# Attended blocks turned on VectorE instead of passing through DRAM, in a sliding-window transformer block

## The chip, the cores and the metric

The kernel runs on one core of a Trainium2 chip. A core has TensorE for matrix products (PE in the profile, PEld for its weight loads), VectorE (DVE), ScalarE (ACT), GpSimd (POOL) and SyncE (SP), which issues most transfers. Sixteen DMA engines move the data. The engines run their own instruction streams in order and wait for each other through semaphores. The metric is the device time of one execution in microseconds; three runs of the kernel before gave 324.6, 325.6 and 327.06 us, a median of 325.6.

## The reference

One block of a transformer with 2048 tokens of 640 features, everything in bf16. A small condition vector `c` gives six vectors of shift, scale and gate:

```python
mod = (_silu(c) @ w_mod).reshape(c.shape[0], 6, 1, -1)
sa, ca, ga, sb, cb, gb = (mod[:, i] for i in range(6))
h = _layernorm(x, axis=-1) * (1 + ca) + sa
x = x + ga * _A_ref(h, A_wqkv, A_wo)
h = _layernorm(x, axis=-1) * (1 + cb) + sb
x = x + gb * _B_ref(h, B_w_gate, B_w_up, B_w_down)
```

`_A_ref` is attention with 32 heads of 20 features. A query sees itself and the 255 keys before it:

```python
qkv = (x @ wqkv).reshape(B, S, 3, H, Dh).transpose(2, 0, 3, 1, 4)
scores = jnp.einsum('bhqd,bhkd->bhqk', q, k) * Dh ** (-0.5)
mask = (idx[:, None] - idx[None, :] >= 0) & (idx[:, None] - idx[None, :] < 256)
p = softmax(where(mask, scores, -1e9))
o = jnp.einsum('bhqk,bhkd->bhqd', p, v)
return o.transpose(0, 2, 1, 3).reshape(B, S, D) @ wo
```

`_B_ref` is a gated MLP with 1536 hidden features: `(sigmoid(x @ w_gate) * (x @ w_up)) @ w_down`.

## The kernel before

The tokens are worked on in 8 chunks of 256, each of two blocks of 128 rows. A chunk `a` goes through these steps:

- `ln1` norms its rows and brings them into `hT`, features on partitions. For chunks 0 and 1 the turn is made on TensorE (line 686, operand `ident`), from chunk 2 on by a DMA that transposes (line 810). The modulation by `ca` and `sa` follows on ScalarE, VectorE or GpSimd (lines 819 to 828).
- `qkv` multiplies `hT` by wq, wk and wv (line 686). Copies out of PSUM (`evac`, lines 902 and 903) put queries and keys into `stg` with each head of 20 padded to 32 columns, and values into `V` with a stride of 22, the last two columns being ones. `stg` is turned into `QT` and `KT`, on TensorE for chunks 0 and 1, else by DMA.
- `attention` runs over two halves `q` of 16 heads. A set of scores (line 687, `S<-QT,KT`) fills four PSUM banks, ScalarE takes the exponential (`L1054`, `L1028`), GpSimd clears what lies outside the window (`L1032`, `L1059`, `L1063`). A PV product (`burst`, line 687, `M<-E,V`) gives two PSUM banks with 16 heads of 20 features and the sum of weights as row 20, heads on partitions in groups of 32. It is issued ahead of a later set of scores, with one half's delay (`pend`).
- `close` ends a half. `norm` (line 1146) turns both banks into `T1` in 32 x 32 blocks on VectorE (L1150), takes reciprocals (L1155), divides into `Tn` (L1157), and turns `Tn` back into `On` (L1159), heads on partitions. Heads of 20 rows in groups of 32 are not the dense 128 rows that the output product needs. So four DMAs write `On` to a DRAM tensor `doc` and one DMA reads `doc` back into `oT`, tiles 0 and 1 after the first half, 2 to 4 after the second.
- `outproj` multiplies `oT` by `wo` (line 686, `M<-wo,oT`), adds the residual (L1240), norms, turns by DMA into `h2T` and modulates. `wo` had been multiplied by the gate `ga` beforehand (L1331), `wd` by `gb` (L1268).
- `mlp` is gate and up products (`M<-h2T,wg` and `M<-h2T,wu`), tanh on ScalarE (L1285), the product on VectorE (L1287), and the down product (`M<-wd,hh`), residual (L1306) and store.

The order of the work is fixed beforehand. Every operation is recorded by `A(...)` with its engines, a cost and the tiles that it reads and writes. `PLAN` is a list of numbers: a number divided by 5 is the operation's place in the recording, the remainder its engine (PE, ACT, DVE, POOL, SP). `schedule` walks the list once, checks that what an operation needs has come before, gives tiles their buffers and keeps each engine's order as listed. `emit` writes the five streams with their semaphores. The costs in microseconds in the calls decide only which buffer a tile takes; a search that is not part of the kernel made the list. All transfers but a few that are listed for ScalarE's queue are issued by SP in its listed order, so one that waits holds those behind it.

Buffers matter to the change: `Tn`, `On`, `T1`, `Dr` and `oT` have one buffer each, and PSUM tiles `M` have four banks. Tn's padding is cleared once on GpSimd (L599).

Of the kernel before, what the change touches and what calls it, by code (L numbers as in the profile page):

```python
# [348 lines left out]
def c_pe(n):  # L349
# [118 lines left out]
]  # L468
TR1 = 2
NPH = 2  # L470
NPQ = 2
PQ = ()
# [913 lines left out]
```

## Time and profile before

| | |
|---|---|
| runs of the kernel before | 324.6, 325.6, 327.06 us |
| the profiled execution | 326.74 us |
| its span, first to last instruction | 324.8 us |
| granted TensorE clock | 1.0 |
| TensorE busy | 316.1 us (97%) |
| ScalarE, VectorE, GpSimd busy | 213.0, 205.6, 188.0 us |
| DMA traffic | 38.20 MB, of that HBM read 21.30 and written 5.25 |

A line of a group reads: line of the kernel, engine, operation, tile written <- tiles read, shapes, count, then busy microseconds and the mean nanoseconds of one, then the engine's idle time before these instructions and what ended it. A wait reads: who waited, for whom, microseconds in total, times, the longest. A stretch reads: from, to, length, then for each engine its busy time and its number of instructions. A row of the timeline or of the chain begins with its start and its length. SPq and ACTq are issues of transfers on a queue.

### The profile page before, as it was taken

The page shows a single profiled execution, that of the slowest core. Times are in us where ns is not written, and L with a number is a line of the kernel's source. Part 1 is how long each engine was busy: PE and PEld are TensorE (multiplying, and loading weights), DVE is VectorE, ACT ScalarE, POOL GpSimd, SP SyncE. Part 2 cuts the span into 40 slices and gives each one's busy share as a digit, 9 for nine tenths or more (in the row PEclk, how much of TensorE's full clock was granted, in tenths as well). Part 3 has the DMA queues.
Part 4 walks back from the last instruction along what each step waited for, and adds up shares of the span by engine and source line. Part 5 has one row for each costly group of instructions (what it writes and reads, how often), then busy time and mean ns, then how long its engine had stood idle before and what let it go on. Part 6 is the DMA issues. An engine that isn't in the chain of part 4 may idle for free.

```text
span 324.8 us, 11997 instructions
## 1 busy us (share of the span) xinstructions
PE 316.1 (97%) x5044; PEld 236.8 (73%) x5045; DVE 205.6 (63%) x426; ACT 213.0 (66%) x228; POOL 188.0 (58%) x349
## 2 busy tenths in 40 slices
PE   6999999989999999999999999999999999999996
PEld 2666767667776777776787777777888777887885
DVE  4699987768686865674755647464845376645423
ACT  2699984788678877988685857676886756320220
POOL 5337858855868677948774846676583958001000
PEclk9999999999999999999999999999999999999999
DMA  7999989998648464726551303465121206112201
GB/s 238 370 315 245 281 161 189 207 192 281 186 91 140 64 139 75 109 60 130 118 71 26 83 2 73 126 65 120 39 47 28 77 22 83 38 46 41 83 0 42
DMA packets 73023, 38.20 MB, mean 118 GB/s; under 512 B 46602, under 2 KB 71690, under 8 KB 72970
## 3 DMA queue, kind: packets, MB, share of 16 engines
q1 hardware_dynamic: 71808, 36.13, 50.6%
q10 hardware_dynamic: 1162, 1.31, 1.5%
q8 instruction: 40, 0.66, 0.9%
q14 instruction: 13, 0.11, 0.1%
HBM read 21.30 MB, written 5.25 MB: 82 GB/s over the span
## 4 chain that ended last, share of the span: by engine, by line
PE 76%; DVE 0%; issue 0%
PE M L686 64%; PE S L687 6%; PE M L687 5%; DVE x L1306 0%
## 5 line engine op out<-in xcount | busy, mean ns | idle before, releaser
L1054 ACT ACTIVATE E<-S 128x2048 bf16<-128x2048 f32 x56 | 105.0, 1876 | 45.7 <-PE S L687 45.4
L1063 POOL TENSOR_SCALAR_AFFINE_SELECT E<-E 128x512 bf16<-128x512 bf16 x112 | 69.6, 635 | 8.4 <-DVE Tn L1157 2.1
L1059 POOL TENSOR_SCALAR_AFFINE_SELECT E<-E 128x256 bf16<-128x256 bf16 x112 | 45.4, 415 | 48.3 <-PE M L686 14.8
L686 PE MATMUL M<-h2T,wu 128*128 128x256 bf16 x480 | 68.0, 273 | 0.5 <-DVE h2T L828 0.5
L686 PE MATMUL M<-h2T,wg 128*128 128x256 bf16 x480 | 67.0, 273 | 0.0
L686 PE MATMUL M<-wd,hh 128*128 128x320 bf16 (+2 forms) x396 | 57.3, 296 | 0.0
L1287 DVE SCALAR_TENSOR_TENSOR hh<-sig,M 128x512 bf16<-128x512 f32 x48 | 32.2, 680 | 34.9 <-ACT sig L1285 24.1
L686 PEld LDWEIGHTS M<-h2T,wu 128*128 128x128 bf16 x480 | 45.3, 98 | 8.4 <-issue 0.7
L686 PEld LDWEIGHTS M<-h2T,wg 128*128 128x128 bf16 x480 | 45.5, 98 | 6.9 <-DVE T L1150 0.2
L686 PEld LDWEIGHTS M<-wd,hh 128*128 128x128 bf16 x396 | 37.0, 98 | 14.0 <-DVE hh L1287 0.2
L1285 ACT ACTIVATE sig<-M 128x512 f32<-128x512 f32 x48 | 28.2, 596 | 27.7 <-PE M L686 27.1
L1032 POOL TENSOR_SCALAR_AFFINE_SELECT E<-E 128x1024 bf16<-128x1024 bf16 x28 | 31.9, 1144 | 6.8 <-DVE st L781 2.5
L1306 DVE TENSOR_TENSOR x<-M,x 128x320 bf16<-128x320 f32 (+2 forms) x33 | 15.7, 479 | 29.4 <-PE M L686 28.9
L687 PE MATMUL S<-QT,KT 20*64 20x256 bf16 (+5 forms) x1856 | 32.3, 228 | 1.3 <-issue 0.7
L687 PEld LDWEIGHTS S<-QT,KT 20*64 20x64 bf16 (+1 forms) x1856 | 20.0, 100 | 18.4 <-issue 8.8
L781 DVE BATCH_NORM_STATS2 st<-x 128x6 f32<-128x320 bf16 x64 | 28.9, 477 | 1.3 <-DMA x<-in_A_x_dram 1.0
L1150 DVE STREAM_TRANSPOSE T<-M 128x512 f32<-128x512 f32 x32 | 21.4, 698 | 13.1 <-PE S L687 10.5
L1028 ACT ACTIVATE E<-S 128x2048 bf16<-128x2048 f32 x14 | 26.3, 1876 | 5.1 <-PE S L687 5.0
L686 PE MATMUL M<-wq,hT 128*128 128x320 bf16 x160 | 25.9, 300 | 1.5 <-ACT hT L827 0.9
L686 PE MATMUL M<-wv,hT 128*128 128x320 bf16 x160 | 26.8, 300 | 0.0
L686 PE MATMUL M<-wk,hT 128*128 128x320 bf16 x160 | 26.2, 300 | 0.0
L686 PE MATMUL M<-wo,oT 128*128 128x320 bf16 x160 | 24.8, 300 | 0.0
(86 smaller groups left out, 362.7 us busy)
## 6 DMA issues: line engine op xcount, KB each, us to landing
x<-in_A_x_dram SPq DMA_DIRECT2D x19, 160.0 KB, 8.4
doc<-On SPq DMA_DIRECT2D x64, 40.0 KB
out_dram<-x SPq DMA_DIRECT2D x14, 160.0 KB, 1.8
wd<-in_w_mod_dram SPq DMA_DIRECT2D x6, 320.0 KB
wd<-in_B_w_down_dram SPq DMA_DIRECT2D x4, 480.0 KB
wu<-in_w_mod_dram SPq DMA_DIRECT2D x5, 320.0 KB
oT<-doc SPq DMA_DIRECT2D x8, 192.0 KB
wg<-in_B_w_gate_dram SPq DMA_DIRECT2D x2, 576.0 KB
```

Source lines behind the costliest of these rows:

```text
L686: return e.matmul(o, l, r, start=st, stop=sp, skip_group_check=True)
L687: return e.matmul(o, l, r, start=st, stop=sp, tile_position=tp, skip_group_check=True)
L781: A("dve", lambda e, g, bi=bi, j=j: e.bn_stats(v(bi * 12 + j * 6, 6), src[bi].ap[:, j * 320:(j + 1) * 320]), 0.48, reads=[src[bi].r()], wr ...
L1028: A("act", lambda e, eng: e.activation(cell().rearrange("p m (x c) -> p m x c", c=64)[:, :, 0:4:3, :], Sp.ap[:].rearrange("p j (k x c) -> ...
L1032: A("pool", lambda e, eng, c0=c0, pat=pat, base=base, cm=cm: e.affine_select(cell()[:, :, c0:c0 + 64], cell()[:, :, c0:c0 + 64], pattern=p ...
L1054: A("act", lambda e, eng: e.activation(part(0, 512), Sp.ap[:], ACT.Exp, scale=SM_SCALE), 1.876, reads=[Sp.r()], writes=[E.r("C"), E.r("B") ...
L1059: A("pool", lambda e, eng, hc=hc, src=src, far_h=far_h: e.affine_select(side(hc), part(src, 64), pattern=[[0, 4], [-1 if far_h else 1, 64] ...
L1063: A("pool", lambda e, eng, c0=c0, near=near: e.affine_select(part(c0, 128), part(c0, 128), pattern=[[0, 4], [1 if near else -1, 128]], com ...
L1150: A("dve", lambda e, g, h=h: e.transpose(T1.ap[:, 512 * h:512 * h + 512], X[h].ap), 0.694, reads=[X[h].r()], writes=[T1.r(h)], prio=3.5, t ...
L1285: A("act", lambda e, g, pg=pg, sg=sg: e.activation(sg.ap[:], pg.ap[:], ACT.Tanh, scale=0.5), c_act(512), reads=[pg.r()], writes=[sg.r()], ...
L1287: A("dve", lambda e, g, pu=pu, sg=sg, f0=f0: e.scalar_tensor_tensor(out=hh.ap[:, f0:f0 + 2, :], in0=sg.ap[:].rearrange("p (a b) -> p a b", ...
L1306: A("dve", lambda e, g, ps=ps, bi=bi, c0=c0, n=n: e.tensor_tensor(x1[bi].ap[:, c0:c0 + n], ps.ap[:, 0:n], x1[bi].ap[:, c0:c0 + n], op=ALU. ...
```

## The change

`On`, `doc`, the four writes and the read of each half go. A half now only turns, takes reciprocals and divides; the divide writes into one `Tn` of 1280 columns for the whole chunk, ordered by block of 32 queries, then head, then feature, without padding. After the second half two turns on VectorE, one for each block of 128 rows, write straight into `oT`. For this the heads are dealt differently: head `16q + 4j + k` lies in partition group `j`, so that the 160 features of a group are five dense tiles of 32 rows. The copies of queries and keys into `stg` write the heads in this order, and `wo` is loaded with its rows permuted alike, by eight DMAs in place of one. The output product waits for `oT` by block of rows and for `wo` by tile. The clearing of `Tn` goes. The costs of `ends` and `score` change, and `PLAN` is a new list that differs from about the tenth microsecond on: 2089 operations instead of 2163.

```diff
 PLAN = [
...
-TR1 = 2
...
-    p_Tn = sbpool("Tn", 1, [128, 1024])
-    p_On = sbpool("On", 1, [128, 1024])
+    p_Tn = sbpool("Tn", 1, [128, 1280])
...
-    for i in range(len(p_Tn.aps)):
-        p_Tn.init[i].append(A("pool", lambda e, g, i=i: e.memset(p_Tn.aps[i][:], 0.0), 1.0, writes=[R("ti")], prio=3))
...
-    dma(lambda: wo[:], lambda: A_wo.rearrange("(t p) f -> p t f", p=128), 2.15, writes=[R_wo], prio=0.5, tag="wo")
+    for t in range(NDT):
+        if t == 2:
+            for j in range(4):
+                dma(lambda j=j: wo[32 * j:32 * j + 32, 2, :],
+                    lambda j=j: A_wo.rearrange("(u e) f -> u e f", e=16)[5 * j + 4:5 * j + 21:16], 0.11, writes=[R_wo[2][j]], prio=0.5,
+                    tag="wo")
+        else:
+            dma(lambda t=t: wo[:, t, :],
+                lambda t=t: A_wo.rearrange("(q j e) f -> q j e f", q=2, j=4)[t // 3][:, (32 * t) % 80:(32 * t) % 80 + 32, :], 0.43,
+                writes=R_wo[t], prio=0.5, tag="wo")
...
-                        evac(lambda s=s, half=half: heads(s.ap[:, half * 512:half * 512 + 512], 32)[:, :, 0:DH],
-                             lambda ps=ps: heads(ps.ap[:, 0:320], DH), 320, [ps.r()], [s.r(half)], 6, f"evqk{a}")
+                        evac(lambda s=s, half=half: s.ap[:, half * 512:half * 512 + 512].rearrange(
+                            "p (k j x) -> p j k x", k=4, x=32)[:, :, :, 0:DH],
+                             lambda ps=ps: ps.ap[:, 0:320].rearrange("p (j k d) -> p j k d", j=4, d=DH), 320, [ps.r()], [s.r(half)], 6, f"evqk{a}")
...
-        last["s"] = [with_pv(f"ends{a}", sc, 0.29, set_reads(a, q), [G, Sp], before, 1)]
+        last["s"] = [with_pv(f"ends{a}", sc, 0.25, set_reads(a, q), [G, Sp], before, 1)]
...
-        last["s"] = [with_pv(f"score{a}", sc, 0.25, set_reads(a, q), [E, Sp], before, 3)]
+        last["s"] = [with_pv(f"score{a}", sc, 0.262, set_reads(a, q), [E, Sp], before, 3)]
...
-                        h = 4 * (4 * q + k) + j
+                        h = 16 * q + 4 * j + k
...
-    def norm(X, On, a):
-        T1, Tn, Dr = Tile(p_T1, "T1"), Tile(p_Tn, "Tn"), Tile(p_Dr, "Dr")
+    def norm(X, Tn, q, a):
+        T1, Dr = Tile(p_T1, "T1"), Tile(p_Dr, "Dr")
...
-        A("dve", lambda e, g: e.tensor_tensor(blk(Tn), blk(T1), Dr.ap[:].unsqueeze(2).to_broadcast([128, 32, DH]), op=ALU.mult),
-          0.82, port=True, reads=[T1.r(0), T1.r(1), Dr.r()], writes=[Tn.r()], prio=4, tag=f"divide_{a}")
-        A("dve", lambda e, g: e.transpose(On.ap[:], Tn.ap[:]), 1.22, reads=[Tn.r()], writes=[On.r()], prio=4, tag=f"tr2_{a}")
+        A("dve", lambda e, g: e.tensor_tensor(
+            Tn.ap[:].rearrange("p (b k d) -> p k b d", k=8, d=DH)[:, 4 * q:4 * q + 4],
+            T1.ap[:].rearrange("p (k b r) -> p k b r", k=4, r=32)[:, :, :, 0:DH],
+            Dr.ap[:].rearrange("p (k b) -> p k b", k=4).unsqueeze(3).to_broadcast([128, 4, 8, DH]), op=ALU.mult),
+          0.82, port=True, reads=[T1.r(0), T1.r(1), Dr.r()], writes=[Tn.r(q)], prio=4, tag=f"divide_{a}")
...
-            On = Tile(p_On, f"On{a}_{q}")
-            norm(X, On, a)
-            for j in range(4):
-                Rj = R(f"doc{a}_{q}_{j}")
-                dma(lambda j=j, q=q: rdoc[j * DH:(j + 1) * DH, 4 * q:4 * q + 4, :],
-                    lambda j=j, On=On: On.ap[32 * j:32 * j + DH, :].rearrange("p (g c) -> p g c", g=4), 0.22,
-                    reads=[On.r()], writes=[Rj], prio=1, tag=f"n_ow_{a}", dur=0.42)
-                R_doc[q].append(Rj)
-            t0, t1 = ((0, 2), (2, 5))[q]
-            dma(lambda t0=t0, t1=t1: oT.ap[:, t0:t1, :], lambda t0=t0, t1=t1: doc.rearrange("(t p) c -> p t c", p=128)[:, t0:t1, :],
-                0.41, reads=R_doc[0] + (R_doc[1] if q else []), writes=[oT.r(q)], prio=1.5, tag=f"oT_{a}", dur=0.5, dlat=2.88)
+            norm(X, Tn, q, a)
             if q == 1:
+                for bi in range(2):
+                    A("dve", lambda e, g, bi=bi: e.transpose(
+                        oT.ap[:, :, bi * 128:bi * 128 + 128].rearrange("p t (b c) -> p b t c", c=32), Tn.ap[:, 640 * bi:640 * bi + 640]),
+                      0.83, reads=[Tn.r(0), Tn.r(1)], writes=[oT.r(bi)], prio=4, tag=f"tr2_{a}")
...
-                pe_chain(ps, 320, pairs, [[oT.r(0 if t < 2 else 1), R_wo] for t in range(NDT)], 15, f"wo{a}",
+                pe_chain(ps, 320, pairs, [[oT.r(bi)] + R_wo[t] for t in range(NDT)], 15, f"wo{a}",
...
-          reads=[R_wo, R_gbc], writes=[R_wo], prio=20, tag="wos")
+          reads=R_wo[t] + [R_gbc], writes=R_wo[t], prio=20, tag="wos")
```

More of the change, by code (lines that the diff above doesn't have):

```diff
@@ L562, in build @@
     R_w3 = {k: [R(k + "0"), R(k + "1")] for k in ("wq", "wk", "wv")}
-    R_crow, R_ident, R_ccol, R_cth, R_siluc, R_silubc, R_wo = (R(n) for n in ("crow", "ident", "ccol", "cth", "siluc", "silubc", "wo"))
+    R_crow, R_ident, R_ccol, R_cth, R_siluc, R_silubc = (R(n) for n in ("crow", "ident", "ccol", "cth", "siluc", "silubc"))
+    R_wo = [[R(f"wo{t}{i}") for i in range(4 if t == 2 else 1)] for t in range(NDT)]
     R_wg = [[R(f"wg{t}_{h}") for t in range(NDT)] for h in range(2)]
@@ L1130, in pv @@
                     for j in range(4):
-                        h = 4 * (4 * q + k) + j
+                        h = 16 * q + 4 * j + k
                         ins = mm(e, X[bank].ap[32 * j:32 * j + 32, oc:oc + n * 128], V[2 * a + kb].ap[:, h * VW:h * VW + 32],
@@ L1144, in burst @@
         return a, pv, (6 if a else 3) * 512 / 2400.0 * 1.04 + 0.02, rd, X
-    def norm(X, On, a):
-        T1, Tn, Dr = Tile(p_T1, "T1"), Tile(p_Tn, "Tn"), Tile(p_Dr, "Dr")
-        blk = lambda t: t.ap[:].rearrange("p (b r) -> p b r", r=32)[:, :, 0:DH]
-        for h in range(2) if TR1 == 2 else ():
+    def norm(X, Tn, q, a):
+        T1, Dr = Tile(p_T1, "T1"), Tile(p_Dr, "Dr")
+        for h in range(2):
             A("dve", lambda e, g, h=h: e.transpose(T1.ap[:, 512 * h:512 * h + 512], X[h].ap), 0.694, reads=[X[h].r()],
               writes=[T1.r(h)], prio=3.5, tag=f"tr1_{a}")
-        if TR1 == 1:
-            A("dve", lambda e, g: e.transpose(T1.ap[:], Mall[:, X[0].slot:X[0].slot + 2, :].rearrange("p a c -> p (a c)")), 1.23,
-              reads=[X[0].r(), X[1].r()], writes=[T1.r(0), T1.r(1)], prio=3.5, tag=f"tr1_{a}")
         A("dve", lambda e, g: e.reciprocal(Dr.ap[:], T1.ap[:, DH:1024:32]), 0.35, reads=[T1.r(0), T1.r(1)], writes=[Dr.r()],
           prio=4, tag=f"recip_{a}")
-        A("dve", lambda e, g: e.tensor_tensor(blk(Tn), blk(T1), Dr.ap[:].unsqueeze(2).to_broadcast([128, 32, DH]), op=ALU.mult),
-          0.82, port=True, reads=[T1.r(0), T1.r(1), Dr.r()], writes=[Tn.r()], prio=4, tag=f"divide_{a}")
-        A("dve", lambda e, g: e.transpose(On.ap[:], Tn.ap[:]), 1.22, reads=[Tn.r()], writes=[On.r()], prio=4, tag=f"tr2_{a}")
+        A("dve", lambda e, g: e.tensor_tensor(
[3 more added lines that the diff above has]
+          0.82, port=True, reads=[T1.r(0), T1.r(1), Dr.r()], writes=[Tn.r(q)], prio=4, tag=f"divide_{a}")
     pend = []
@@ L1176, in attention @@
     def attention(a):
-        doc = dram(f"doc{a}", [D, CH])
-        rdoc = doc.rearrange("(g r) c -> r g c", r=4 * DH)
-        R_doc = [[], []]
-        oT = Tile(p_oT, f"oT{a}")
+        oT, Tn = Tile(p_oT, f"oT{a}"), Tile(p_Tn, f"Tn{a}")
         def close(q, X):
-            On = Tile(p_On, f"On{a}_{q}")
-            norm(X, On, a)
-            for j in range(4):
-                Rj = R(f"doc{a}_{q}_{j}")
-                dma(lambda j=j, q=q: rdoc[j * DH:(j + 1) * DH, 4 * q:4 * q + 4, :],
-                    lambda j=j, On=On: On.ap[32 * j:32 * j + DH, :].rearrange("p (g c) -> p g c", g=4), 0.22,
-                    reads=[On.r()], writes=[Rj], prio=1, tag=f"n_ow_{a}", dur=0.42)
-                R_doc[q].append(Rj)
-            t0, t1 = ((0, 2), (2, 5))[q]
-            dma(lambda t0=t0, t1=t1: oT.ap[:, t0:t1, :], lambda t0=t0, t1=t1: doc.rearrange("(t p) c -> p t c", p=128)[:, t0:t1, :],
-                0.41, reads=R_doc[0] + (R_doc[1] if q else []), writes=[oT.r(q)], prio=1.5, tag=f"oT_{a}", dur=0.5, dlat=2.88)
+            norm(X, Tn, q, a)
             if q == 1:
+                for bi in range(2):
+                    A("dve", lambda e, g, bi=bi: e.transpose(
+                        oT.ap[:, :, bi * 128:bi * 128 + 128].rearrange("p t (b c) -> p b t c", c=32), Tn.ap[:, 640 * bi:640 * bi + 640]),
+                      0.83, reads=[Tn.r(0), Tn.r(1)], writes=[oT.r(bi)], prio=4, tag=f"tr2_{a}")
                 x1, h2 = outproj(a, oT)
```

223 rows, old and new, of the table PLAN are left out of this document.

## The prediction

> **What bounds the kernel now.** I read the page first: busy shares, clock, and the chain that ended last.
>
> ```profile
> PE 316.1 (97%) x5044; PEld 236.8 (73%) x5045; DVE 205.6 (63%) x426; ACT 213.0 (66%) x228; POOL 188.0 (58%) x349
> PEclk9999999999999999999999999999999999999999
> DMA  7999989998648464726551303465121206112201
> PE 76%; DVE 0%; issue 0%
> ```
>
> TensorE (PE) is busy 97% of 324.8 us at full clock, and the chain that ended last is TensorE for 76% of the span. That leaves 324.8 - 316.1 = 8.7 us (8.66 by the stretches) without a matmul, and the first question is where those lie. The chain in order of time gives its start and its end; stretches of 8 us give the rest.
>
> ```profile
> 76.36 0.05 issue
> ...
> 277.92 44.28 PE M L686 x384
> ...
> 322.22 0.29 DVE x L1306
> ```
>
> ```profile
> 0.00:8.00 8.00, 5.36 (x29) 2.09 (x30) 3.23 (x11) 1.96 (x3) 4.24 (x19) 1.00 0.73 237
> 8.00:16.00 8.00, 7.39 (x91) 5.23 (x90) 5.02 (x16) 4.87 (x12) 2.95 (x12) 1.00 1.09 370
> 16.00:24.00 8.00, 7.91 (x100) 5.45 (x98) 7.42 (x19) 7.53 (x10) 2.87 (x7) 1.00 0.98 319
> 32.00:40.00 8.00, 7.73 (x172) 5.78 (x169) 7.42 (x15) 7.42 (x9) 7.14 (x9) 1.00 0.96 264
> 40.00:48.00 8.00, 7.28 (x124) 4.86 (x123) 6.41 (x15) 6.99 (x11) 4.12 (x8) 1.00 0.92 185
> 64.00:72.00 8.00, 7.07 (x104) 4.58 (x106) 5.74 (x13) 6.79 (x10) 5.63 (x12) 1.00 1.21 207
> 72.00:80.00 8.00, 7.40 (x187) 5.88 (x180) 6.54 (x14) 6.29 (x8) 3.08 (x6) 1.00 0.86 268
> 320.00:324.80 4.80, 2.18 (x25) 1.71 (x23) 1.54 (x4) 0.00 (x0) 0.00 (x0) 1.00 0.24 72
> ```
>
> Columns are TensorE, weight loads, VectorE, ScalarE, GpSimd, then clock, DMA share and GB/s. TensorE's idle time: 2.64 us before 8 us, 0.61 up to 16, then 0.09 + 0.27 + 0.72 + 0.93 + 0.60 = 2.61 in the stretches shown between 16 and 80, and 2.62 at the end. The rest, 8.66 - 8.48 = 0.2, lies in the three stretches left out. From 80 to 320 us every stretch reads 8.00. So **the only time that an order or a shorter path can win lies before 80 us: 0.61 + 2.8, about 3.4 us**. Up to 72 us the DMA engines are full too (share 0.92 to 1.21). TensorE's waits name what is late there:
>
> ```profile
> PE M L686 <- DVE x L803: 1.3, 1, 1.3
> PE M L686 <- ACT hT L827: 0.9, 1, 0.9
> PE S L687 <- issue: 0.7, 1, 0.7
> PE M L686 <- DVE h2T L828: 0.5, 1, 0.5
> PE M L686 <- DVE hT L820: 0.5, 1, 0.5
> ```
>
> By their sizes they fit the stretches: 0.9 the one from 64 us (hT of a later chunk, turned by DMA and then modulated on ScalarE), 0.5 for h2T the one from 72 us (again a turn by DMA), 0.7 "issue", which has no releaser, the one from 40 us; 1.3 and the 0.5 for hT L820 lie before 16 us, where chunk 0 is normed. Is TensorE at its peak where it shows 100%? Starts tell it, since ends are modelled:
>
> ```profile
> 289.76 2.88 PE L686 MATMUL M<-wo,oT 128*128 128x320 bf16 x20
> ...
> 292.47 0.82 PE L686 MATMUL M<-h2T,wu 128*128 128x256 bf16 x6
> ```
>
> Twenty matmuls of 320 columns go in 292.47 - 289.76 = 2.71 us, 135 ns each; 320 columns in 135 ns is 2.37 columns per ns. The last 44.28 us hold 384 matmuls of 256 and 320 columns, 115 ns each. I read that as packed.
>
> The Trainium skill (Perfetto Trace Analysis, Identifying the Most-Contended Engine) says that matmul busy time is no measure of distance to the roofline, and weight-load busy share is; by its rule the 73% above would leave a quarter of the span to a better order. By the starts of the rows the gap is not there to be had; the rival below gives what it would make.
>
> **The change, part by part.** The groups that carry the prices:
>
> ```profile
> L1150 DVE STREAM_TRANSPOSE T<-M 128x512 f32<-128x512 f32 x32 | 21.4, 698 | 13.1 <-PE S L687 10.5 <-PE M L687 2.3
> L1159 DVE STREAM_TRANSPOSE On<-Tn 128x1024 bf16<-128x1024 bf16 x16 | 19.9, 1242 | 0.4
> L1157 DVE TENSOR_TENSOR Tn<-T,Dr 128x640 bf16<-128x640 f32 x16 | 13.4, 838 | 0.3
> L743 DVE STREAM_TRANSPOSE mt<-M 128x160 f32<-128x160 f32 x2 | 0.7, 334 | 0.0
> L903 DVE CAST stg<-M 128x320 bf16<-128x320 f32 x35 | 16.4, 485 | 12.1 <-PE M L686 12.1
> L903 DVE CAST V<-M 128x320 bf16<-128x320 f32 x21 | 9.9, 478 | 3.0 <-PE M L686 2.9
> ```
>
> *Second turn on VectorE.* Before: two per chunk of 1024 elements, 2 x 1242 = 2.48 us. After: two of 640. Between 160 elements (334 ns) and 1024 (1242) one element costs 908/864 = 1.05 ns, so 640 cost 334 + 480 x 1.05 = 838 ns, 1.68 us per chunk. Eight chunks: 8 x 0.8 = **6.4 us of VectorE saved**. None of it is on the chain: VectorE is busy 63% and TensorE did not wait for it beyond 80 us. Only in 16 to 40 us, where VectorE is busy 7.42 of 8, would it count; there chunk 0's second turn of the first half (1.24) now comes later, with the chunk's second half.
>
> *Divide and projection copies* keep their elements and their runs of 20; only the order of the runs changes. The new strides have no row. Lower end: no change, since the copy into V (stride 22) costs 478 against 485 into stg (stride 32). Upper end: the dearest element of a turn, 698/512 = 1.36 ns, for 640 of them 0.87 us instead of 0.84, on 16 divides and 16 turns 1 us. I take the lower end, the row of the same kind of write; either end falls on an engine that is idle for 37% of the span.
>
> *The way through DRAM* goes: per half chunk four writes and one read.
>
> ```profile
> doc<-On SPq DMA_DIRECT2D x64, 40.0 KB
> oT<-doc SPq DMA_DIRECT2D x8, 192.0 KB
> L576 SPq DMA_DIRECT2D doc<-On x64: 280/343/1244, 35.3 to 282.9; - x64
> L576 SPq DMA_DIRECT2D oT<-doc x16: 382/390/1059, 41.4 to 284.7; - x16
> SPq L576 <- DVE On L1159: 65.7, 14, 13.9
> ```
>
> SP loses 64 x 0.34 + 16 x 0.39 (the medians) = 28 us of issuing and the 65.7 us for which it stood in front of On, with loads and turns queued behind. Before 60 us lie chunk 0's eight writes and two reads, 8 x 40 + 320 = 640 KB (what is written is read again), at the 185 to 207 GB/s of the stretches there **3.1 to 3.5 us of full DMA engines**. What that is worth is read from a turn by DMA under load and without:
>
> ```profile
> 66.84 2.52 SPq L810 DMA_TRANSPOSE h2T<-x  x2
> 73.50 0.60 ACT L827 ACTIVATE h2T<-h2T,shB,scB 128x256 bf16<-128x256 bf16 x1 [1.17 <-DMA h2T<-x]
> 296.40 2.53 SPq L810 DMA_TRANSPOSE h2T<-x  x2
> 300.42 0.60 ACT L827 ACTIVATE h2T<-h2T,shB,scB 128x256 bf16<-128x256 bf16 x1 [5.84 <-DMA h2T<-x]
> ```
>
> From the end of the issue to the first use 73.50 - 69.36 = 4.1 us under load, 300.42 - 298.93 = 1.5 without. The two TensorE waits on turns by DMA (0.9 and 0.5) and the 0.7 of "issue" are shorter than this difference of 2.6.
>
> *New waits.* The turn into oT waits until the previous chunk's output product has read oT, and blocks VectorE behind it (copies, GLU). In the new list (entry divided by 5 is the operation, the remainder the engine) each chunk's output product stands ahead of the next chunk's second PV product, so this wait is over when it is reached: nothing. Output products now wait per block of 128 rows, 0.84 us apart.
>
> *wo in eight loads instead of one.* Seven more issues on SP, at 0.34 us 2.4 us, against 28 taken off; but in the new list three of them, 480 KB, come ahead of the last piece of wm1, and TensorE's product for the gate waits for that. At 319 GB/s the piece is 1.5 us later; the gate's product stands behind the first PV product now and not ahead of it. If that cover fell short, TensorE would stand still for up to 1.5 us. I take nothing.
>
> *Tn's clearing on GpSimd* goes from the first 8 us, where GpSimd is busy for 4.24: nothing. *The costs 0.25 and 0.262* only feed the order.
>
> *The order.* From 80 us on the old one had no gap, so the new one can only keep that. In its tail, 18 steps of two matmuls stand between the last PV product and the last output product (at 115 ns 4.1 us; 11.8 before, 277.92 to 289.76), for two turns, a divide and one new turn, 1.4 + 0.84 + 0.84 = 3.1 us, and a reciprocal of 32 columns between them. Behind it 20 steps of two and 13 of four (40 x 0.115 + 52 x 0.135 = 11.6 us) cover norm and turn of the last chunk, which took from 292.5 to the 300.4 above and then some modulations of 0.6. Enough: nothing won or lost.
>
> **Sum.** 0.9 + 0.5 + 0.7 = 2.1 us off. The profiled execution took 326.74 us (324.8 span and 1.9 around it) and becomes 324.6; the runs shown have a median of 325.6, 1.1 below it (324.6 to 327.06), so the median becomes **323.5**. What is late next: VectorE and ScalarE, 7.4 to 7.5 of 8 in 16 to 40 us, which feed the first chunks' projections.
>
> **The rivals.**
> - *All gaps before 80 us go.* The order is new from the tenth microsecond and VectorE gets air. Then 3.4 us plus some tenths hidden under modelled ends, 325.6 - 4 = 321.6. For it: every gap has a late feeder that the change relieves. Against: two queues at 93% remain.
> - *Hidden anyway.* No gap names oT or On. Chunk 0's last read is issued 4.9 us ahead of its use:
>
> ```profile
> 47.41 0.38 SPq L576 DMA_DIRECT2D oT<-doc  x1
> ...
> 52.32 2.88 PE L686 MATMUL M<-wo,oT 128*128 128x320 bf16 x20
> ```
>
>   If the waits come from loads that remain, the time is 325.6. Against: 3.3 us of traffic leaves the stretch in which turns land late.
> - *Slower: turns by DMA come late more often.* The new list moves bulk pieces of wg, wd and wo ahead of the turns of chunks 2 to 4 on SP. TensorE runs in order; each late turn costs what the one in the stretch from 64 us did, 0.9 and some tenths hidden under modelled ends. It decides when three or four more are late, that is when a turn's landing grows past the 4.1 us above by 1 us for each: 325.6 + 3.5 = 329.1. For it: DMA share above 1 to 72 us. Against: 3.3 us of traffic gone.
> - *TensorE can be packed tighter.* If matmuls could follow at the pace of their weight loads (98 ns in the row below) and not at 115, the last 384 alone would win 384 x 0.017 = 6.5 us, 319. Against: 135 ns for 320 columns and 115 in the mean follow the columns, not the loads. This is what the Trainium skill's rule above would make of it.
>
> ```profile
> L686 PEld LDWEIGHTS M<-h2T,wg 128*128 128x128 bf16 x480 | 45.5, 98 | 6.9 <-DVE T L1150 0.2
> ```
>
> **How the numbers follow.** Forecast 0.33 (322.4 to 324.8), hidden anyway 0.17 (to 327), all gaps 0.28 (321 to 322.3), slower 0.20 (329 and beyond), tighter 0.02. A measurement here tells about 1% from no change, 3.3 us. Faster by over 1%: 0.28 + 0.02 = 0.30; within 1%: 0.33 + 0.17 = 0.50; slower 0.20. The range from 321.0 to 329.3 leaves out the tighter case and the half of the slower case beyond its price, about 0.12.
>
> **What would show it.** Right: no write to or read from a DRAM copy of the attended block; VectorE's turns at about 0.84 us, VectorE near 199 us; TensorE without waits on hT, h2T and "issue" between 40 and 80 us, the gap-free chain starting earlier than 76 us, and 8.00 in each later stretch. Wrong: a stretch beyond 80 us below 8.00, a strided turn or divide above 1 us, or TensorE waiting for KT, QT or hT more than before.

## The result and the profile after

The kernel after took a median of **331.3 us** (329.0 to 332.6) against 326.3 us (324.6 to 327.2) for the kernel before on the same chip: 1.0148 times as long, 95% interval 1.0105 to 1.0192. The forecast was 323.5 us, with a range from 321.0 to 329.3. The profiled execution took 331.3 us with a span of 329.7 us, 4.9 us more than before.

The page of the kernel after, busy shares, clock, DMA share and the chain that ended last:

```profile
PE 316.3 (96%) x5045; PEld 236.2 (72%) x5045; DVE 200.5 (61%) x430; ACT 211.1 (64%) x222; POOL 191.5 (58%) x350
PEclk9999999999999999999999999999999999999999
DMA  7979699999628265344121500055120203002101
PE 83%; DMA 9%; POOL 4%; DVE 1%; issue 1%; ACT 1%; SPq 0%; DVEq 0%; POOLq 0%; ACTq 0%
```

TensorE has the same work (316.3 against 316.1 us) at full clock, VectorE 5.1 us less. So the whole loss is standing time of TensorE. But the chain now has DMA in it, 9%; the chain before shows none, though it is followed back only to 76.36 us. The stretches of the kernel after (TensorE, weight loads, VectorE, ScalarE, GpSimd, clock, DMA share, GB/s) say where:

```profile
0.00:8.00 8.00, 4.97 (x21) 1.78 (x22) 3.36 (x12) 1.96 (x3) 3.41 (x18) 1.00 0.73 241
8.00:16.00 8.00, 7.50 (x101) 5.43 (x102) 4.75 (x16) 5.28 (x12) 2.76 (x8) 1.00 1.09 369
16.00:24.00 8.00, 8.00 (x99) 5.52 (x96) 7.34 (x20) 7.39 (x11) 2.47 (x9) 1.00 0.68 205
24.00:32.00 8.00, 7.92 (x166) 5.55 (x155) 7.25 (x19) 7.37 (x9) 6.28 (x9) 1.00 1.16 235
32.00:40.00 8.00, 6.36 (x131) 4.54 (x132) 7.07 (x15) 7.24 (x9) 6.71 (x9) 1.00 0.72 206
40.00:48.00 8.00, 7.23 (x139) 4.78 (x130) 4.46 (x10) 4.66 (x6) 2.03 (x4) 1.00 1.03 181
48.00:56.00 8.00, 7.17 (x95) 4.59 (x93) 6.79 (x17) 6.63 (x9) 6.06 (x12) 1.00 1.14 247
56.00:64.00 8.00, 5.48 (x144) 3.87 (x141) 4.72 (x12) 2.75 (x3) 7.42 (x16) 1.00 1.04 163
64.00:72.00 8.00, 7.36 (x102) 4.72 (x95) 4.90 (x12) 7.04 (x8) 3.90 (x6) 1.00 1.23 176
72.00:80.00 8.00, 8.00 (x156) 5.62 (x155) 6.39 (x16) 5.86 (x8) 4.60 (x9) 1.00 0.89 276
80.00:88.00 8.00, 7.52 (x135) 5.71 (x133) 7.19 (x14) 6.60 (x7) 6.08 (x11) 1.00 1.03 251
128.00:136.00 8.00, 7.86 (x186) 5.77 (x185) 6.05 (x12) 4.91 (x4) 4.52 (x8) 1.00 0.18 43
```

Up to 88 us TensorE stands for 10.5 us (the sum of 8 less the TensorE column over the first eleven rows). Before, the rows shown for the prediction with its remainder of 0.2 give 2.64 + 0.61 + 2.61 + 0.2 = 6.1 us. **So 4.4 of the 4.9 us were lost before 88 us**, most of it between 32 and 64 us. Two stretches also show the DMA engines emptier than before: 0.68 at 205 GB/s from 16 to 24 us, where it was 0.98 at 319, and 0.72 at 206 from 32 to 40 us, where it was 0.96 at 264. Less traffic is less to move, but in the second of them transfers were waited for. TensorE's waits, and the pieces of the chain in order of time (start, length):

```profile
PE S L687 <- issue: 3.0, 2, 2.5
PE M L687 <- issue: 1.6, 1, 1.6
PE M L686 <- DVE V L903: 0.8, 1, 0.8
```

```profile
32.07 7.01 DMA gate<-grow
39.10 4.56 DMA gbc<-gate
```

The gate `ga` of 1.2 KB goes to DRAM and comes back spread over 128 partitions. Issued at 32.07, it took 7.01 us to land, and the load of `gbc` could be issued only then, at 39.10; before, the same pair was 29.02 and 33.87, which is 4.85. `PE M L687` is the product with the last piece of `w_mod` (into `wd`). The profile names no releaser for it, but that piece, issued at 32.63 us, took 7.1 us to land, and TensorE went on at 39.81. VectorE's scaling of `wo` waited for `gbc`, with the copies of V behind it, and TensorE for those:

```profile
43.78 0.49 DVE L1321 TENSOR_TENSOR wo<-wo,gbc 128x640 bf16<-128x640 bf16 x1 [2.48 <-DMA gbc<-gate]
```

What was the queue doing meanwhile? The DMA view of the kernel after from 36 to 40 us, in 40 slices (tenths of share, then GB/s), and the issues of `wo`:

```profile
DMA  9999998867645333322222222222322322412422
GB/s 233 246 233 248 274 205 174 174 143 182 156 113 133 97 105 79 120 77 64 96 93 90 102 102 93 90 102 92 113 87 102 118 90 92 189 61 77 156 56 41
```

```profile
L570 SPq DMA_DIRECT2D wo<-in_A_wo_dram x8: 537/626/817, 11.3 to 39.5; - x8
```

From 38 us the share stands mostly at 0.2 to 0.3 and the rate mostly at 90 to 102 GB/s, with work queued. The experiments show what that is.

### The profile page after: what moved, and what is told of

It reads as the page before. It is cut to its first block, busy times and chain, and to the rows that moved or that the text cites. A ratio compares the mean times of both kernels' runs of the same rounds, so it can differ in the third digit from the quotient of the medians.

```text
span 329.7 us, 11862 instructions
## 1 busy us (share of the span) xinstructions
PE 316.3 (96%) x5045; PEld 236.2 (72%) x5045; DVE 200.5 (61%) x430; ACT 211.1 (64%) x222; POOL 191.5 (58%) x350
## 2 busy tenths in 40 slices
DMA packets 61894, 32.95 MB, mean 100 GB/s; under 512 B 45714, under 2 KB 60562, under 8 KB 61842
## 4 chain that ended last, share of the span: by engine, by line
PE 83%; DMA 9%; POOL 4%; DVE 1%; issue 1%; ACT 1%; SPq 0%; DVEq 0%; POOLq 0%; ACTq 0%
PE M L686 69%; PE S L687 7%; PE M L687 6%; POOL E L1064 2%; DMA gate<-grow 2%; DMA hT<-x 2%; DMA wd<-in_w_mod_dram 2%; DMA x<-in_A_x_dram 2%; DMA gbc<-gate 1%; POOL E L1060 1%; ACT E L1055 1%; PE S L686 1%; POOL x L800 0%; SPq L570 0%; DVE wo L1321 0%
## 5 line engine op out<-in xcount | busy, mean ns | idle before, releaser
L1055 ACT ACTIVATE E<-S 128x2048 bf16<-128x2048 f32 x56 | 105.1, 1876 | 37.1 <-PE S L687 36.9
L1064 POOL TENSOR_SCALAR_AFFINE_SELECT E<-E 128x512 bf16<-128x512 bf16 x112 | 71.6, 657 | 10.2 <-DVE wo L1321 5.7
L1060 POOL TENSOR_SCALAR_AFFINE_SELECT E<-E 128x256 bf16<-128x256 bf16 x112 | 47.6, 439 | 50.9 <-ACT E L1055 29.7
L686 PE MATMUL M<-h2T,wu 128*128 128x256 bf16 x480 | 66.2, 273 | 0.0
L686 PE MATMUL M<-h2T,wg 128*128 128x256 bf16 x480 | 65.3, 273 | 0.0
L686 PEld LDWEIGHTS M<-wd,hh 128*128 128x128 bf16 x396 | 37.1, 98 | 13.6
L687 PE MATMUL S<-QT,KT 20*64 20x256 bf16 (+5 forms) x1856 | 32.4, 228 | 3.0 <-issue 3.0
L687 PEld LDWEIGHTS S<-QT,KT 20*64 20x64 bf16 (+1 forms) x1856 | 20.0, 100 | 19.6 <-issue 10.4
L686 PE MATMUL M<-wv,hT 128*128 128x320 bf16 x160 | 27.8, 300 | 0.4 <-DVE stg L903 0.4
L686 PE MATMUL M<-wo,oT 128*128 128x320 bf16 x160 | 26.1, 300 | 0.4 <-DVE wo L1321 0.4
L686 PE MATMUL M<-wq,hT 128*128 128x320 bf16 x160 | 25.2, 299 | 1.1 <-ACT hT L827 0.6
```

Of the source, the lines that this page charges most:

```text
L686: return e.matmul(o, l, r, start=st, stop=sp, skip_group_check=True)
L687: return e.matmul(o, l, r, start=st, stop=sp, tile_position=tp, skip_group_check=True)
L1055: A("act", lambda e, eng: e.activation(part(0, 512), Sp.ap[:], ACT.Exp, scale=SM_SCALE), 1.876, reads=[Sp.r()], writes=[E.r("C"), E.r("B") ...
L1060: A("pool", lambda e, eng, hc=hc, src=src, far_h=far_h: e.affine_select(side(hc), part(src, 64), pattern=[[0, 4], [-1 if far_h else 1, 64] ...
L1064: A("pool", lambda e, eng, c0=c0, near=near: e.affine_select(part(c0, 128), part(c0, 128), pattern=[[0, 4], [1 if near else -1, 128]], com ...
```

## The experiments

The ratio of each is against the kernel before, run beside it on the same chip. The edits are shown shortened, with words in place of longer code. In SyncE's orders `wm`, `wv`, `wg`, `wu`, `wd` and `wo` are loads of weights, `x` and a number a load of a block of rows, `atr` a turn by DMA of `hT`, `qkt` one of `QT` or `KT`; `gout` writes the gate to DRAM and `gin` is the load of `gbc`.

### First run: path and order apart

```diff
 PLAN (kernel after) = [
-  the new order
+  the order of before; writes and reads of doc left out, the two new turns at the place
+  of the second half's turn, the eight loads of wo at the place of the one
```

> The changed kernel's operations in the order of the kernel before: what is gone is left out of its list, the eight loads of wo stand where the one load stood, the two turns into oT where the second half's turn stood. Theory (the loss is the new order's): TensorE's gaps between 16 and 80 us are those of before or less, 2.8 us or under, and the time is 324 to 326.5, at or below the kernel before. Rival (the new path itself costs: strided turns, divides or projection copies, or wo in eight pieces): most of the 5 us stays, 329 to 331, and the waits of after at 38, 43 and 61 us are seen here too.

Measured: 336.7 us, 1.030 (1.025 to 1.035). Slower than both kernels and than either expectation, so the new order isn't the cause; it makes up for something. TensorE's longest wait and the stretches of this run:

```profile
PE M L686 <- DVE stg L903: 6.2, 1, 6.2
```

```profile
32.00:40.00 8.00, 8.00 (x174) 5.99 (x172) 6.68 (x15) 7.72 (x9) 6.06 (x8) 1.00 0.38 80
40.00:48.00 8.00, 4.56 (x83) 2.84 (x81) 2.15 (x4) 4.94 (x6) 1.68 (x1) 0.98 1.26 250
48.00:56.00 8.00, 5.26 (x47) 3.04 (x48) 7.12 (x15) 3.20 (x5) 5.37 (x11) 0.59 0.81 133
```

SyncE needed from 31.3 to 37.1 us to issue the eight loads (31.0 to 31.6 for the one before), so `gbc` was issued at 37.2 instead of 33.9 us and landed 9.0 us later. VectorE's scaling of `wo` waited 5.9 us for it, TensorE behind that. Yet from 32 to 40 us, while the loads were issued, the DMA engines were busy for 0.38, where before they were for 0.96.

### Second: modulation weights ahead

```diff
 SyncE's order in the kernel after
-wv, wo, wo, x6, x5, x7, wm1, wm1, wm1, wo, wm1, wm1, wm2
+wv, wm1, wm1, wm1, wm1, wm1, wo, wo, x6, x5, x7, wo, wm2
```

> The changed kernel; on SP's queue alone the five loads of wm1 (into wu) are moved ahead of three loads of wo and of the load of x that waits for a turned block until 17.3 us. Theory (between 13 and 17 us SP stands in front of that load with little issued behind it, DMA engines run dry, and all later transfers come late): DMA share in 16 to 24 us rises from 0.68 to above 0.9, the wait of 1.6 us at 38 us for the second part of the modulation goes, and gbc's at 43 us shrinks; 2 to 4 us faster than the changed kernel, 327 to 329. Rival (DMA engines are not what holds TensorE up there; VectorE's order is): under 1 us of change.

Measured: 336.3 us, 1.029 (1.024 to 1.035). The rows x5 to x7, issued behind 1.6 MB of w_mod, now took 6.4 us to land (a piece of the chain), and TensorE stood for 2.3 us at 23 us. The DMA share from 16 to 24 us rose to 0.99, as the theory had it, and the time got worse. Whether earlier pieces of `w_mod` would help without the later rows, this run doesn't show.

### Third and fourth: the first loads of wd later, and both moves

```diff
 SyncE's order in the kernel after
-gin, wo, wg0, atr3, atr3, x8, wd, gout, x9, wg0, qkt2 x3, gin, x10, wd, ..., wg1
+gin, wo, wg0, atr3, atr3, x8, gout, x9, wg0, qkt2 x3, gin, x10, ..., wg1, wd, wd
```

> The changed kernel; on SP's queue alone the first two of four loads of wd (480 KB each, first used beyond 100 us) are moved from before 56 us to behind the weights of the MLP. Theory (TensorE's 2.5 us of issue at 61 us is a page of its instructions that stands behind a full set of DMA queues): that gap falls below 1 us and the time by 1.5 to 3 us, 328 to 330. Rival (the gap is set by how densely TensorE's instructions stand, not by traffic): the gap stays at 2 us or more and the time within 1 us of the changed kernel.

> Both moves on SP's queue together. Theory (one cause, transfers ordered badly, and two places): the sum of the two, 4 to 6 us faster than the changed kernel, 325 to 327. Rival: no more than the better of the two alone, since what one frees the next late transfer takes.

Measured: 341.9 us, 1.046 (1.042 to 1.051), and 343.5 us, 1.049 (1.043 to 1.056). The "issue" wait near 61 us is gone in the third run, but TensorE now waits later, for a modulation that stands on VectorE behind the scaling of the late `wd`:

```profile
PE M L686 <- DVE h2T L828: 8.9, 1, 8.9
```

The gap went as the third run's theory said, the time did not; for the fourth, the sum of two gains, there were none to add. What the four runs have in common with the kernel after are the eight loads of `wo`.

### Fifth: eight loads of whole rows

The kernel before, with the load of `wo` cut into eight:

```diff
-    dma(wo[:], A_wo.rearrange("(t p) f -> p t f", p=128))
+    for each t but 2, and four times 32 partitions of t = 2:
+        dma(wo[p0:p1, t, :], A_wo.rearrange("(t p) f -> p t f", p=128)[p0:p1, t, :])
```

> The kernel before, with its order and its way through DRAM, in which only the one load of wo is eight loads at the same place (four of 128 rows, four of 32 rows, same bytes, same layout). Theory (the eight loads hold SyncE's queue, and what stands behind them there, above all the load of gbc, comes late): SyncE issues wo for some 5.5 us instead of 0.57, so the load of gbc is issued at about 37 instead of 33.87 us and lands at 42 to 46 us, the scaling of wo on VectorE waits, TensorE stands for 3 to 6 us near 44 us, and the time is 330 to 337 us. Rival (it is the new path itself, the turn or the order of VectorE, that costs the time): 325 to 328 us, like the kernel before.

Measured: **329.2 us, 1.006 (1.003 to 1.009)**. `gbc` was issued at 36.6 us, as the theory had it, but VectorE did not wait for it. It waited 1.8 us for a write of `On` and 1.3 us for a turn of `hT`, both queued behind the loads, and TensorE stood at 45 and 49 us for 1.1 and 0.9 us, not for 3 to 6. The number of loads costs some 2 us, and that is not enough for what the first run lost.

### Sixth and seventh: the loads elsewhere in the queue

The first run with the eight loads moved: into two pauses of SyncE, or behind `gbc`.

```diff
 SyncE's order in the first run
-wm3, atr2, wu0, gout, atr2, wo x8, gin, x8, x9
+wm3, wo (t 0, 1, 3, 4), atr2, wu0, gout, atr2, wo (t 2) x4, gin, x8, x9
```

> The kernel of the first run (new path, order of before), with the loads of wo moved to two pauses of SyncE's queue: the four loads of 128 rows ahead of the first turn by DMA of hT (the queue paused there from 22.5 to 25.6 us before), the four of 32 rows behind the second one (paused from 31.6 to 33.9 us). Theory: the load of gbc is issued within 1.5 us of the 33.87 us of before and lands before 40.5 us; no stall of more than 2.5 us near 44 us; 324 to 329 us. Rival (the new path itself): 333 us or more, with a stall near 44 us wherever the loads stand.

```diff
-wm3, atr2, wu0, gout, atr2, wo x8, gin, x8, x9
+wm3, atr2, wu0, gout, atr2, gin, wo x8, x8, x9
```

> The kernel of the first run (new path, order of before), with all eight loads of wo behind the load of gbc. Theory: the load of gbc is issued at 33 to 34.5 us and lands at about 39 us as before, but the eight loads are issued until about 39.5 us and the last lands at about 42 us, so that the scaling of wo waits for them for 1 to 4 us; 326 to 332 us, between the kernel before and the first run. Rival (the new path itself): 333 us or more.

Measured: 334.6 us, 1.024 (1.020 to 1.027), and 337.4 us, 1.034 (1.029 to 1.038). The theory of issue time missed both times. In the sixth run the turns by DMA behind the first four loads took 4.3 and 3.7 us to issue, and `gbc` came at 39.9 us; TensorE's longest wait was 4.9 us. In the seventh it was issued at 32.1 us, ahead of everything, but the turns of hT queued behind `wo` landed late, and VectorE waited 8.2 us for one of them. Wherever the loads stand, what is behind them pays. The DMA view of the seventh run from 36 to 41 us, in 40 slices:

```profile
DMA  1211223223232222322224491214212222222222
```

The queue is full of work and the engines are busy for two to three tenths. If each packet only took longer, the share would be high; this looks like few engines, each of them busy. So the next experiment changes the rows of the loads and not their place.

### Eighth: eight loads of blocks

The fifth run with the rows of the kernel after:

```diff
-        dma(wo[p0:p1, t, :], A_wo.rearrange("(t p) f -> p t f", p=128)[p0:p1, t, :])
+        dma(wo[p0:p1, t, :], four blocks of 32 rows 80 apart; for t = 2 two of 16 rows)
```

> The fifth run (kernel before, eight loads of wo) with one thing more: each load takes the rows of wo in the order of the kernel after (four blocks of 32 rows that lie 80 apart, and twice 16 rows for the middle part), so the output product gets the rows of wo in another order than that path wants them in, and only the time counts. Theory (the loads of blocks run on a quarter of the DMA engines: while nothing else was on the queue, the seventh run showed a DMA share of 0.22 to 0.26 and 83 to 97 GB/s, where the kernel before showed 0.98 to 1.07 and 333 to 360): the DMA share is below 0.5 for some 6 us behind 33 us, what is behind wo on the queue lands 4 to 8 us late, TensorE stands for 4 to 8 us between 42 and 52 us, and the time is 333 to 338 us, as in the first run. Rival (eight issues are all that the loads cost): 328 to 330 us, as in the fifth run.

Measured: **334.0 us, 1.020 (1.018 to 1.023)**. The shape of the rows, with nothing else changed, costs 4.8 us against the fifth run. The DMA view from 34 to 40 us, when little else than `wo` was on the queue (slices in tenths, GB/s, packets and share of the queue):

```profile
DMA  1122122122222222222222421222322372222332
GB/s 34 60 77 77 68 77 77 68 94 102 94 102 94 102 102 102 94 94 102 94 102 94 85 68 51 68 85 94 123 77 102 94 195 85 94 85 102 85 85 102
q1 hardware_dynamic: 415, 0.51, 25.1%
```

The eight loads of whole rows in the fifth run, from 34 to 38 us, with some other transfers among them:

```profile
DMA  7999995999993675445213551056978997889754
q1 hardware_dynamic: 928, 0.88, 75.0%
```

And of the kernel before from 34 to 36 us, behind its one load:

```profile
DMA  0499989999999989999999989999999889999999
GB/s 0 128 358 410 384 282 307 358 384 384 410 384 384 358 282 333 358 358 410 384 384 410 333 256 358 358 384 410 358 410 384 282 282 410 333 410 410 358 283 384
q1 hardware_dynamic: 557, 0.69, 102.4%
```

The packets themselves are no slower: 0.251 x 16 x 6 us / 415 = 58 ns of an engine for each, 1.024 x 16 x 2 us / 557 = 59 ns before. A full queue moves 384 to 410 GB/s, 24 to 25.6 for each of 16 engines. Four engines make 96 to 102: just what the loads of four blocks show, at a share of 0.25. So **a load whose rows come as four blocks runs on four of the sixteen engines**. The four large loads, 655 KB, take 655 / 98 = 6.7 us so, and what is queued behind them on those four engines waits: `gbc`, issued at 37.8 us, let VectorE go on at 46.5. The Trainium skill (DMA: Bandwidth & Descriptors, Why a DMA increments its semaphore by 16 and not by 1) says that a transfer takes the largest number of engines up to 16 that divides the slowest dimension (leaving out those of size one) of both its sides; with 4 blocks against 128 partitions that is 4. The trace agrees.

TensorE's wait that came of it, and the stretch behind it:

```profile
PE M L693 <- DVE stg L910: 6.7, 1, 6.7
```

```profile
48.00:56.00 8.00, 4.70 (x43) 2.67 (x44) 6.26 (x14) 2.83 (x5) 5.78 (x11) 0.57 0.92 157
```

### Ninth to eleventh: the same rows by loads that spread

In the first run and in the kernel after, the large loads are cut by blocks of rows instead of by column tile: 64 neighbouring rows go to 32 partitions and two tiles, so that the outermost dimension is 32.

```diff
-    for t in (0, 1, 3, 4): dma(wo[:, t, :], four blocks of 32 rows, 80 apart)
+    for t0 in (0, 3): for j in range(4):
+        r0 = (t0 // 3) * 320 + 80 * j + (16 if t0 else 0)
+        dma(wo[32 * j:32 * j + 32, t0:t0 + 2, :], A_wo[r0:r0 + 64].rearrange("(t e) f -> e t f", t=2))
```

> The first run (new path, order of before) with the same rows of wo brought to the same places by twelve loads: eight of 64 neighbouring rows (32 partitions by two column blocks) and the four of twice 16 rows. Theory of the DMA engines: the eight loads move at the rate of the one load of before; the DMA share in 32 to 40 us goes from 0.38 back to 0.7 or more, the stall of 6.35 us near 44 us falls below 2.5 us, and the time is 326 to 331 us although SyncE issues four loads more. Rival (it is the number of issues or the new path itself): 336 us or more, for twelve issues take longer than eight.

> The kernel after, in its own order, with the twelve loads in place of the eight, at their places. Theory of the DMA engines: the load of gbc, which was issued at 39.10 us, is issued by 37 us, the DMA share in 36 to 40 us goes from 0.47 to 0.7 or more, TensorE's stalls before 64 us lose 1.5 to 3 us, and the time is 327 to 330 us. Rival (it is the order, with SyncE's pause from 12.8 to 17.3 us, that costs): 331 us or more.

> The ninth run with five of its twelve loads in SyncE's pause ahead of the first turn by DMA of hT, three behind the second, and the four of the middle part behind the load of gbc. Theory of the DMA engines, with the pauses for cover: the load of gbc is issued at 33 to 35 us; 324 to 328 us, at or below the kernel before. Rival (the new path itself costs): 333 us or more.

Measured: 334.1 us, 1.020 (1.015 to 1.024); **327.4 us, 1.002 (0.998 to 1.006)**; 331.9 us, 1.013 (1.010 to 1.017). In the order of the kernel after, the spread loads give back 3.9 us, and the kernel is level with the one before. Its stretches:

```profile
32.00:40.00 8.00, 8.00 (x197) 5.78 (x194) 6.91 (x16) 6.98 (x8) 6.59 (x9) 1.00 0.94 244
40.00:48.00 8.00, 8.00 (x122) 5.36 (x106) 6.86 (x15) 7.78 (x9) 4.54 (x8) 1.00 1.08 240
48.00:56.00 8.00, 7.69 (x153) 5.52 (x152) 6.26 (x16) 5.12 (x8) 6.73 (x14) 1.00 1.07 189
56.00:64.00 8.00, 5.27 (x89) 3.47 (x88) 3.80 (x10) 4.51 (x5) 5.57 (x10) 1.00 1.30 164
```

From 32 to 48 us TensorE has no gap any more (2.4 us in the kernel after), the DMA share from 32 to 40 us is 0.94 instead of 0.72, and `gbc` is issued at 35.8 instead of 39.1 us, 4.1 us behind the gate. In the order of before the twelve loads miss what was expected: 336.7 to 334.1 us, with the stall near 44 us down from 6.2 to 3.7 and not below 2.5, though the DMA share from 32 to 40 us rose to 0.71, as expected. In the pauses `gbc` is issued at 35.3 us, and the time is 4 us above what was expected. Twelve loads in one place keep SyncE for 8.4 us, and the four of twice 16 rows are narrower still. The DMA view of the first of the three from 38 to 40 us, when only their data moved:

```profile
DMA  0020000000011111101111111111030001011111
GB/s 26 26 26 0 0 0 26 26 26 26 26 51 51 51 51 51 51 26 51 51 51 51 51 51 51 51 51 51 26 51 26 26 26 51 26 51 51 51 51 51
```

51 GB/s at a tenth of the share is two engines, for two blocks; 26 is one.

### Twelfth and thirteenth: all loads spread, and the last stall

```diff
-    for j in range(4): dma(wo[32 * j:32 * j + 32, 2, :], twice 16 rows, 320 apart)
+    for j in range(4): for q in range(2):
+        dma(wo[32 * j + 16 * q:32 * j + 16 * q + 16, 2, :], A_wo[320 * q + 80 * j + 64:320 * q + 80 * j + 80])
 SyncE's order: these eight behind wv, in the pause from 12.8 to 17.3 us
```

> The tenth run (kernel after, its own order, eight loads of wo of 64 neighbouring rows) with the middle part, too, in loads of neighbouring rows: eight of 16 rows in place of four of twice 16, all in SyncE's pause that ran from 12.8 to 17.3 us in the kernel after. Theory (the four loads of twice 16 rows run on two DMA engines: in the ninth run the DMA share stood at 0.09 to 0.22 with 32 to 62 GB/s from 37 to 40 us, while only they were moved): the DMA share in 32 to 40 us stays at 0.9 or more, the load of gbc is issued at 35 to 36 us, and the time is that of the tenth run or up to 1.5 us less, 325.5 to 328.5 us. Rival (sixteen issues are too many for SyncE): 329 us or more.

Measured: **326.0 us, 0.997 (0.994 to 1.001)**, as the theory had it, although SyncE issues sixteen loads. The DMA share from 32 to 40 us was 0.82 in its profiled execution (329.2 us, 3.2 above the median), not the 0.9 expected.

```diff
 SyncE's order in the run before this
-gin, x10, wd, qkt2, qkt3, atr4, atr4, qkt3
+gin, x10, qkt2, qkt3, atr4, atr4, wd, qkt3
```

> The twelfth run with the second load of wd behind SyncE's next turns by DMA (two of QT and KT, two of hT) instead of ahead of them. TensorE's stall of 2.7 us at 57 us in the tenth run, for which the profile names only the issue, begins while those turns wait for 5.1 us behind the second load of wd. Theory: the stall comes from the full queue (TensorE's next instructions are read through the same DMA engines), so with the load moved the stall is below 1 us and the time is 1 to 3 us below the twelfth run, 323 to 326.5 us. Rival: wd then comes late for VectorE's scaling, and the stall moves to behind 68 us: 327 to 335 us.

Measured: **325.9 us, 0.996 (0.993 to 0.999)**, the best of all kernels here, 1.0 us below the one before. TensorE's waits from 16 to 90 us, which were 2.7 us of "issue" and some more in the tenth run:

```profile
PE S L687 <- issue: 1.0, 1, 1.0
PE M L686 <- DVE stg L903: 0.2, 1, 0.2
```

The stall near 57 us is gone, and nothing came behind 68 us but the 1.0 us at 80 us. But the 1 to 3 us below the twelfth run did not come: the two medians are 0.1 us apart, and the twelfth run's profiled execution, without this move, has no "issue" wait above 0.8 us. So whether that stall is instructions read late through a full queue stays open.

## Why the prediction was wrong, step by step

- **What bounds the kernel** held. TensorE's work stayed 316 us, each stretch from 88 to 320 us reads 8.00 as before but one with 7.86, and 4.4 of the 4.9 us lost lie before 88 us.
- **The second turn** was sized rightly: 838 ns forecast, 830 measured (the second row below); VectorE went from 205.6 to 200.5 us, where 199 was forecast. 0.8 us of the difference is the divide, whose new stride costs 886 ns and not 838, just above the upper end named (0.87) and not the lower that was taken: 16 x 48 ns. The copies into `stg` kept their price, 484 against 485 ns; the rest is work that the new list deals out differently. None of it was on the path.

```profile
L1154 DVE TENSOR_TENSOR Tn<-T,Dr 128x640 bf16<-128x640 f32 x16 | 14.2, 886 | 0.2
L1182 DVE STREAM_TRANSPOSE oT<-Tn 128x640 bf16<-128x640 bf16 x16 | 13.1, 830 | 0.2
```

- **New waits: nothing.** Right: VectorE's idle time ahead of the new turns is 0.2 us in all, as the second row says.
- **The way through DRAM** is gone, 38.20 to 32.95 MB. That fits the 640 KB priced for a chunk, eight times 5.1 MB. The 207 GB/s of the faster end is a stretch from 64 us on; those from 40 to 64 us had 182 to 192, so 3.3 to 3.5 us. What was missed is that something else in the same change holds up what the freed engines could have moved.
- **wo in eight loads: "I take nothing."** This is the step that failed. Its issues were priced at 0.34 us each (0.63 measured, 5.0 us in all), its transfers at 319 GB/s. The step counted bytes and issues, and asked which piece comes ahead of which; it did not ask how many engines a load runs on. 655 KB went at about 98 GB/s and 164 KB at about 51. The term should have been 3.9 us for the large loads (331.3 less 327.4, one change alone; 4.2 by the two ratios) and up to 1.4 us for the small ones (327.4 less 326.0; the intervals overlap, so this one is not settled). The largest price that the step names, 1.5 us, is less than half of that.
- **The sum** of 0.9 + 0.5 + 0.7 took three waits off whole. With all loads spread, the measured gain is 0.9 to 1.0 us, less than half of it. Only the thirteenth run's interval (0.993 to 0.999) leaves out no change at all, and that run also moves a load of `wd`; so what the shorter path alone is worth is not shown. "Issue" and a turn of hT still cost 2.7 and 1.0 us in the tenth run. That is nearer to the rival "hidden anyway" than to the forecast.
- **The order** "can only keep" the dense part: right but for 0.5 us from 80 to 88 us and 0.1 from 128, which the prediction had named as a sign of being wrong. The new list did more than keep it: with the loads as they are it is worth some 5 us against the old one (336.7 to 331.3). It scatters the narrow loads between 11 and 40 us instead of issuing them in one go. That the scattering is what helps was not tried apart.
- **The slower rival** had the side, at 329.1 us, but not the mechanism: the loads of wo cost by the few engines they run on, not by bulk ahead of the turns. Moving the first two loads of `wd` far back made things worse (third run), moving the second behind the next turns changed nothing measurable (thirteenth).

A rule that spoke against the change stood in the Trainium skill's page named above, and the diff held what it needs, four blocks outermost in the source of `wo`. As a rival from rows it would have read: 655 KB at a quarter of the 333 to 360 GB/s of the kernel before, 7.3 to 7.9 us instead of 2, the gate's way through DRAM behind it.

## What to carry to other kernels

When a load's access pattern changes, look at the count of its outermost dimension before its bytes: a permuted load of the same size can hold a quarter of the engines three to four times as long, and everything queued behind it pays. Cut such a load so that 32 neighbouring rows are outermost, as in the tenth run (16 in the twelfth), even if that is more loads. In the profile the sign is a DMA share that stands at a simple fraction (0.25, 0.125) and a rate in the same proportion while transfers are waited for; a mean over 8 us can hide it (0.72 in the kernel after from 32 to 40 us), slices of 0.1 us show it.

## What the runs showed of the hardware

Narrow loads also slow the issuer: eight issues of blocks took 6.4 us on SyncE, eight of whole rows at the same place 5.0.

A stall costs more than its length. Behind the one of 6.7 us in the eighth run the granted clock was 0.57 from 48 to 56 us (row above), behind the 8.9 us of the third run 0.50. A stretch of the eleventh run, with a stall of 2.5 us in it:

```profile
48.00:56.00 8.00, 5.50 (x38) 2.94 (x39) 4.92 (x13) 4.15 (x6) 4.23 (x9) 0.68 0.88 167
```

Behind the 2.3 us of the second run the clock was 0.79 from 24 to 32 us. In the kernel after, 2.5 us at 61 us left it at 1.00 (rows from 56 to 72 us above), and so did the 2.7 us of the tenth run. The Trainium skill (TensorE: Matmul & The Clock Gate, Part 1: The HAM clock gate) has the clock fall to a half after an idle window of about 3.4 us. That agrees with the long stalls. That 2.5 us did it in one run and not in another is not what a fixed 3.4 us would give, and the measurement decides: in these runs a stall of 2.3 to 2.7 us went either way, and why stays open.
